# Decode attention beside a GEGLU FFN on one core: cache tiles of four heads in 64 KB rows, two overlapping key places and one value place

## The chip, the cores and the metric

The kernel runs on one core of a Trainium2 chip. The metric is the device time of one execution in microseconds (us). Before the change it is 1317.43 us, the median of three runs (1317.10 to 1317.47). A core has a matmul engine (PE, with its weight loads shown apart as PEld), a vector engine (DVE), an activation engine (ACT), a general engine (POOL) and a queue engine (SP) which here issues every transfer. Sixteen DMA engines carry a transfer together, each its own share of the rows. SBUF is the on-chip memory of 128 partitions, PSUM the small memory that PE writes.

## What is computed

One decode step with a batch of 4: attention over a cache, beside a gated FFN, mixed by a gate. Everything is float32.

```
q  = (x @ wq) as (4, 32 heads, 128)           # x: 4 x 512, wq: 512 x 4096
s  = q . k_cache / sqrt(128)                  # k_cache: 4 x 32 x 4096 x 128
p  = softmax(s)                               # over the 4096 cached positions
a  = (p . v_cache as 4 x 4096) @ wo           # v_cache like k_cache, wo: 4096 x 512
b  = (gelu_tanh(x @ w_gate) * (x @ w_up)) @ w_down    # F = 1792
g  = sigmoid(sum(x * gate_w))
out = g * a + (1 - g) * b                     # 4 x 512
```

The two caches are 268 MB each. All weights together are 28 MB. Every byte is read once.

## The kernel before

**Tiles.** A tile of the cache is two heads (`HT = 2`) of one batch row: 2 x 4096 positions x 128 numbers, 4 MiB. It lies as 128 partitions of 32 KB; a partition holds `R = 64` consecutive positions of one head, which are one contiguous run in memory. There are `NT = 64` key tiles and 64 value tiles. Group `g` is the pair of heads, `b = i % 4` the batch row of tile `i`.

**Buffers.** A pool `kv` of `NB = 5` buffers of 32 KB per partition holds everything that is streamed: `wq` (two halves), key and value tiles, the FFN's weights and `wo`. `load` (L62 to L79) takes the next buffer and issues one transfer on SP, so a transfer waits until the last reader of what lay in that buffer five loads earlier is done. The list `loads` (L81 to L86) fixes the order: `wq` halves, key 0, then key `i+1` and value `i` in turn. `w_gate` and `w_up` come behind values 19 and 20 (`FFN_AT = 20`), `wo`'s first half ahead of the last three value tiles, `w_down` and `wo`'s second half (in three pieces, `WO_END`) at the very end.

**One tile's work (main loop, L310 to L347).** Keys: DVE multiplies the tile by the query, spread over all partitions (`products`, L190, in two halves of 128 x 4096 numbers), and sums each position's 128 products (`sums`, L194); then it takes the maximum of each partition (`max_a`, L201) and PE turns that column into a row (L203). One tile later `soft_max` (L206 to L217) takes the maximum of each head (L208), spreads it with a small matmul (L210), and ACT computes the exponentials into `PM` (L215), an array with zeros around the weights of each head. `pv` (L228) multiplies values by these weights on PE: 16 matmuls of 128 x 512, each of which runs as two passes, into a PSUM tile `PO`. After four tiles `gather` (L240) copies `PO`, sums its parts and the denominators with small matmuls; `weigh` (L253) divides; once per 16 heads `turn` and `turned` (L261, L269) bring the result into the layout that `project_a` (L278) multiplies with `wo`.

**Order.** The schedule is written by hand: each engine runs its instructions in program order, and each waits for semaphores of the others. In tile `i` the program takes the next load of the list after `sums(i)` and again after `pv(i-1)`; each is issued once its buffer is free. `ffn_up` and `ffn_gelu` run inside tiles 20 and 21, `project_a(0)` in tile 62. After the loop come the last softmax and `pv`, `gather`, `weigh`, `turn`, `turned`, `ffn_down` with `w_down`, `project_a(1)` with `wo`'s second half, the mixing by the gate (L360) and the store (L361).

**Start.** PE needs `x` and the first half of `wq` for the queries (L147); DVE picks each partition's head and batch row from the result (L162 to L166), `q_spread` (L174) spreads a group's query over the partitions.

Of the kernel before, what the change touches and what calls it, by code (L numbers as in the profile page):

```python
# [17 lines left out]
def tile_gated_mix(ctx: ExitStack, tc: tile.TileContext, x, kc, vc, wq, wo, w_gate, w_up, w_down, gate_w, out):  # L18
    nc = tc.nc
# [6 lines left out]
    HT = 2  # L26
    PH = P // HT
    R = S // PH
    NT = B * H // HT
    NB = 5  # L30
    TW = R * D
    RJ = 4
    RA = R // 2
    FFN_AT = 20
# [3 lines left out]
    E = HW * D // P  # L38
    WO_END = (0, 10, 14, E)
# [7 lines left out]
    sel = head.tile([P, RJ, B, HT], F32)  # L47
    t1 = head.tile([P, E * B], F32)
    qd = head.tile([P, D], F32)
    xT = head.tile([P, KC, 4, B, 8], F32)  # L50
    kv = ctx.enter_context(tc.tile_pool(name="kv", bufs=NB))
# [7 lines left out]
    T = {}  # L59

    def load(kind, i):
        t = T[kind, i] = kv.tile([P, TW], F32, name="kv")  # L62
        if kind in "kv":
            h, b = HT * (i // B), i % B
            src = (kc if kind == "k" else vc)[b, h:h + HT].rearrange("h (p r) d -> (h p) (r d)", p=PH)
            n = 2 if (kind, i) == ("v", NT - 1) else 1
            for s in range(n):
                nc.sync.dma_start(t[:, s * TW // n:(s + 1) * TW // n], src[:, s * TW // n:(s + 1) * TW // n])
        elif kind == "q":
            nc.sync.dma_start(t, wq.rearrange("(p c) n -> p (c n)", c=KC)[:, i * TW:(i + 1) * TW])  # L70
        elif kind == "f":
            nc.sync.dma_start(t[:, :KC * F], (w_gate, w_up)[i].rearrange("(p c) n -> p (c n)", c=KC))
        elif kind == "d":
            nc.sync.dma_start(t[:, :FC * DM], w_down.rearrange("(p i) n -> p (i n)", i=FC))
        else:
            src = wo[i * HW * D:(i + 1) * HW * D].rearrange("(p e) n -> p (e n)", e=E)
            ends = WO_END if i else (0, E)
            for e0, e1 in zip(ends, ends[1:]):
                nc.sync.dma_start(t[:, e0 * DM:e1 * DM], src[:, e0 * DM:e1 * DM])  # L79

    loads = [("q", 0), ("q", 1), ("k", 0)]  # L81
    for i in range(NT - 2):
        loads += [("k", i + 1), ("v", i)]
        if i in (FFN_AT - 1, FFN_AT):
            loads.append(("f", i - FFN_AT + 1))
    loads[-1:] = [("k", NT - 1), ("w", 0)] + [("v", i) for i in range(NT - 3, NT)] + [("d", 0), ("w", 1)]  # L86
    loads = iter(loads)

    def load_next():
        n = next(loads, None)  # L90
        if n:
            load(*n)

    load_next()
    x_sb = consts.tile([B, DM], F32)
    nc.sync.dma_start(x_sb, x.rearrange("b s d -> (b s) d"))
    load_next()
    for _ in range(NB - 2):
        load_next()
# [5 lines left out]

    for j in range(RJ):
        nc.vector.tensor_reduce(sel[:, j], ident.rearrange("p (c b m) -> p b m c", c=4, b=B)[:, :, HT * j:HT * (j + 1), :],
                                axis=AX.X, op=OP.add)


    PZ = 32 - RJ * HT
# [15 lines left out]
    def gate():  # L127
        z = ps2.tile([P, 1], F32, name="sm")
        for c in range(KC):
            nc.tensor.matmul(z, xT[:, c, :], gw[:, c:c + 1], start=c == 0, stop=c == KC - 1)  # L130
        ez = work.tile([P, 1], F32, name="m1")
        nc.scalar.activation(ez, z, AF.Exp, scale=-1.0)
        gd = work.tile([P, 1], F32, name="nb")
# [8 lines left out]
    for c in range(KC):  # L142
        w = T["q", c // 2].rearrange("p (c n) -> p c n", c=2)[:, c % 2, :]
# [6 lines left out]
    u = consts.tile([P, 2, 512], F32)  # L150
# [9 lines left out]
    nc.vector.tensor_reduce(hmask, ident.rearrange("p (j b a) -> p j a b", j=4, b=B), axis=AX.X, op=OP.add)  # L160
    for s in range(2):
        nc.vector.tensor_tensor(u[:, s].rearrange("p (a d) -> p a d", d=D), PO[s],  # L162
                                amask[:, s * HB:(s + 1) * HB, None].to_broadcast([P, HB, D]), op=OP.mult)
# [4 lines left out]
    for _ in range(2):  # L168
        load_next()
# [17 lines left out]
    def products(i, r0, r1):  # L187
        g, b = divmod(i, B)
        t = T["k", i].rearrange("p (r d) -> p r d", d=D)[:, r0:r1]
        nc.vector.tensor_tensor(t, t, QB[g][:, b:b + 1, :].to_broadcast([P, r1 - r0, D]), op=OP.mult)  # L190

    def sums(i):
        SC[i] = work.tile([P, R], F32, name="sc")
        nc.vector.tensor_reduce(SC[i], T["k", i].rearrange("p (r d) -> p r d", d=D), axis=AX.X, op=OP.add)  # L194

# [32 lines left out]
    def pv(i, j0=0, j1=R // RJ):  # L228
        g, b = divmod(i, B)
        N, n = RJ * D, R // RJ  # L230
        for j in range(j0, j1):
            c, m0 = j % 4, PZ + 32 * j - RJ * HT * b
            nc.tensor.matmul(PO[g % 2][32 * c:32 * c + 32].rearrange("p j d -> p (j d)"), PM[i % 2][:, m0:m0 + 32],  # L233
                             T["v", i][:, j * N:(j + 1) * N], start=b == 0 and j < 4, stop=b == B - 1 and j >= n - 4)

    OS, OT = {}, {}

    def gather(g):  # L240
        o = work.tile([P, RJ, D], F32, name="o", bufs=1)
        nc.scalar.activation(o, PO[g % 2], AF.Copy)  # L242
        OS[g] = ps2.tile([B * HT, D + 1], F32, name="sm")
        for j in range(RJ):
            nc.tensor.matmul(OS[g][:, :D], sel[:, j].rearrange("p b h -> p (b h)"), o[:, j, :],  # L245
                             start=j == 0, stop=j == RJ - 1)
# [3 lines left out]

    ONA = consts.tile([B * HT, E, HW // HT, HT, D // E], F32)

    def weigh(g):  # L253
        ri = work.tile([B * HT, 1], F32, name="ri")
        nc.vector.reciprocal(ri, OS[g][:, D:])  # L255
        nc.vector.tensor_scalar(ONA[:, :, g % (HW // HT)],  # L256
                                OS[g][:, :D].rearrange("p (k e) -> p e k", e=E)[:, :, None, :]
# [3 lines left out]
    def turn(w):  # L261
        OT[w] = ps1.tile([P, E, B, HT], F32, name="oT")
        for e in range(E):
            nc.tensor.transpose(OT[w][:, e].rearrange("p b h -> p (b h)"), ONA[:, e].rearrange("q g h k -> q (g h k)"),  # L264
                                ident[:B * HT, :B * HT])

    OTS = {}

    def turned(w):  # L269
        t = work.tile([P, E * B, HT], F32, name="tm", bufs=1)  # L270
        nc.vector.tensor_tensor(t, OT[w].rearrange("p e b h -> p (e b) h"),
                                pmask[:, None, :].to_broadcast([P, E * B, HT]), op=OP.mult)
        nc.vector.tensor_tensor(t1, t[:, :, 0], t[:, :, 1], op=OP.add)
        OTS[w] = work.tile([P, E, 32], F32, name="ot", bufs=1)
        nc.scalar.activation(OTS[w].rearrange("p e (b k) -> p (e b) k", k=8), t1[:, :, None].to_broadcast([P, E * B, 8]),
                             AF.Copy)

    def project_a(w):  # L278
        for e in range(E):
            project(a_acc, OTS[w][:, e, :], T["w", w][:, e * DM:(e + 1) * DM], (w, e) == (0, 0),  # L280
# [3 lines left out]
    hT = consts.tile([P, FC, 32], F32)  # L284

    def ffn_up(s):
        ps = ps1.tile([P, FG], F32, name="q")
        for c in range(KC):
            for j in range(4):
                nc.tensor.matmul(ps[32 * j:32 * j + 32, :], xT[:, c, :32],  # L290
                                 T["f", s][:, c * F + j * FG:c * F + (j + 1) * FG], start=c == 0, stop=c == KC - 1)
        nc.scalar.activation(u[:, s, :FG], ps, AF.Copy)

    def ffn_gelu():
        x1 = u[:, 0, :FG]
        s = T["f", 1].rearrange("p (a n) -> p a n", n=512)
        t1, t2, t3, th, y, v = (s[:, a, :FG] for a in range(6))
# [5 lines left out]
        nc.vector.scalar_tensor_tensor(v, y, 0.5, u[:, 1, :FG], op0=OP.mult, op1=OP.mult)  # L303
# [4 lines left out]
    def ffn_down():  # L308
        w = T["d", 0].rearrange("p (f n) -> p f n", n=DM)
        for f in range(FC):  # L310
            project(b_acc, hT[:, f, :], w[:, f, :], f == 0, f == FC - 1)


    q_spread(0)
    for i in range(NT):
        g, b = divmod(i, B)
        pair = i > B and i % B == 1
        products(i, 0, RA)
        if i > 0:
            soft_max(i - 1)  # L320
        if pair:
            weigh(g - 1)
        products(i, RA, R)
        sums(i)
        load_next()
        if i > 0:
            pv(i - 1)
            load_next()
# [3 lines left out]
        if pair and g % (HW // HT) == 0:  # L332
            turn(g // (HW // HT) - 1)
            turned(g // (HW // HT) - 1)
        if i == 2:
            nc.sync.dma_start(gw, gate_w.rearrange("(p c) -> p c", c=KC))
        if i == 6:
            gate()
        if i + B < NT and b == 1:
            q_spread(g + 1)  # L340
        if i in (FFN_AT, FFN_AT + 1):
            ffn_up(i - FFN_AT)
            if i == FFN_AT + 1:
                ffn_gelu()
            load_next()
        if i == NT - 2:
            project_a(0)  # L347
            load_next()
# [9 lines left out]
    project_a(H // HW - 1)  # L358
# [25 lines left out]
```

## Time and profile before

| | before |
|---|---|
| median of three runs | 1317.43 us |
| profiled execution, its own time | 1317.39 us |
| span of the profiled execution, first to last instruction | 1315.5 us |
| instructions | 7385 |
| read from HBM | 564.67 MB |
| DVE busy | 1165.0 us (89%) |
| PE busy | 500.1 us (38%) |
| ACT busy | 90.5 us (7%) |
| granted PE clock, mean | 0.651 |

The page of the profile cuts the span into 40 slices with a digit for each engine's busy share. It lists the DMA queues, the chain of work that ended last (each step followed back to what released it), and the costliest groups of instructions with the mean duration and the idle time before them. Other views are the timeline of a stretch (start, duration, engine, line, operation, and in brackets the idle time of the engine before it and what ended that), the waits of an engine or of SP's queue, and the DMA part for a stretch. Times in the text are from the start of the span.

### The profile page before, as it was taken

The numbers are of one execution on the slowest core, as the hardware profiler recorded it, in microseconds if no ns is written. First come the engines' busy times: TensorE is split into PE (matmuls) and PEld (weight loads), VectorE is DVE, ScalarE is ACT, GpSimd is POOL, SyncE is SP. The second block draws the span as 40 slices with busy tenths as digits, with TensorE's granted clock in tenths as the row PEclk, the third lists the DMA queues.
The fourth block names the chain that finished last, engine by engine and source line by source line (L and its number), as shares of the span: only waits on it lengthen the run. The fifth ranks groups of instructions, "written<-read, shape, count | busy, mean of one in ns | idle before, by whom it ended". The sixth has DMA issues, their size and how long they took to land.

```text
span 1315.5 us, 7385 instructions
## 1 busy us (share of the span) xinstructions
PE 500.1 (38%) x3004; PEld 164.5 (13%) x3004; DVE 1165.0 (89%) x402; ACT 90.5 (7%) x359; POOL 0.7 (0%) x6
## 2 busy tenths in 40 slices
PE   3243443343334334334425433443433432442326
PEld 0011111011111111101111111111111110110113
DVE  2999999999999689999999999999999999999963
ACT  0000000000000000000000000000000000000001
POOL 0000000000000000000000000000000000000000
PEclk9556766666676766566566566657657666666658
DMA  9999999999999999999999999999999999999997
GB/s 410 435 430 430 430 433 438 435 430 431 431 434 434 437 431 432 430 434 435 432 434 430 431 434 435 434 432 430 431 434 433 437 429 430 434 434 433 431 430 334
DMA packets 20076, 565.14 MB, mean 430 GB/s; under 512 B 2360, under 2 KB 2376, under 8 KB 2508
## 3 DMA queue, kind: packets, MB, share of 16 engines
q1 hardware_dynamic: 20044, 564.69, 99.5%
q8 instruction: 23, 0.38, 0.1%
q14 instruction: 9, 0.07, 0.0%
HBM read 564.67 MB, written 0.01 MB: 429 GB/s over the span
## 4 chain that ended last, share of the span: by engine, by line
DMA 61%; DVE 36%; PE 2%; issue 1%; ACT 0%; SPq 0%; DVEq 0%; ACTq 0%
DMA kv<-in_A_k_cache 58%; DVE sc L194 17%; DVE kv L190 17%; DMA kv<-in_A_v_cache 2%; PE po L233 1%; DVE m L201 0%; DVE m L208 0%; PE q L290 0%; PE a_acc L226 0%; DVE ONA L256 0%; PE b_acc L226 0%; PE oT L264 0%; PE sm L203 0%; PE q L178 0%; DVE hT L306 0%
## 5 line engine op out<-in xcount | busy, mean ns | idle before, releaser
L190 DVE TENSOR_TENSOR kv<-kv,qb 128x4096 f32<-128x4096 f32 x128 | 564.8, 4413 | 76.4 <-DMA kv<-in_A_k_cache 76.4
L194 DVE TENSOR_REDUCE sc<-kv 128x64 f32<-128x8192 f32 x64 | 555.9, 8686 | 6.3
L233 PE MATMUL po<-kv,pm 128*32 128x512 f32 x2048 | 372.2, 892 | 283.6 <-DMA kv<-in_A_v_cache 277.7
L210 PE MATMUL sm<-m,ones 1*128 1x2 f32 x128 | 37.1, 357 | 320.4 <-DVE m L208 320.4
L233 PEld LDWEIGHTS po<-kv,pm 128*32 128x32 f32 x2048 | 92.4, 155 | 506.9 <-issue 500.5
L203 PE MATMUL sm<-ident,m 128*1 128x128 f32 x64 | 19.0, 297 | 175.3 <-DVE m L201 175.1
L210 PEld LDWEIGHTS sm<-m,ones 1*128 1x128 f32 x128 | 31.6, 305 | 352.2 <-DVE m L208 346.5
L212 ACT ACTIVATE nb<-sm 128x2 f32<-128x2 f32 x64 | 11.0, 172 | 803.3 <-PE sm L210 803.3
L215 ACT ACTIVATE pm<-sc,nb 64x64 f32<-64x64 f32 x128 | 44.5, 348 | 3.0 <-ACT nb L212 0.2
L203 PEld LDWEIGHTS sm<-ident,m 128*1 128x1 f32 x64 | 5.1, 79 | 223.2 <-issue 121.5
L208 DVE TENSOR_REDUCE m<-sm 1x2 f32<-1x128 f32 x64 | 17.4, 272 | 13.1 <-PE sm L203 13.1
L178 PE MATMUL q<-QM,hmask 128*64 128x512 f32 x64 | 25.4, 885 | 3.4 <-DVE QM L166 3.4
L182 ACT ACTIVATE qb<-q 128x512 f32<-128x512 f32 x16 | 9.6, 597 | 226.6 <-PE q L178 226.6
L215 ACT ACTIVATION_READ_ACCUMULATOR pm<-sc,nb 64x1 f32 x128 | 23.6, 185 | 0.0
L245 PE MATMUL sm<-o,sel 128*8 128x128 f32 x128 | 16.6, 273 | 11.4 <-ACT o L242 11.4
L242 ACT ACTIVATE o<-po 128x512 f32<-128x512 f32 x16 | 9.6, 597 | 141.4 <-PE po L233 141.4
L201 DVE TENSOR_REDUCE m<-sc 128x1 f32<-128x64 f32 x64 | 14.1, 220 | 2.2
L245 PEld LDWEIGHTS sm<-o,sel 128*8 128x8 f32 x128 | 10.2, 89 | 28.6 <-ACT o L242 26.8
L255 DVE RECIPROCAL ri<-sm 8x1 f32<-8x1 f32 x16 | 2.3, 147 | 10.1 <-PE sm L247 10.1
L147 PE MATMUL po<-kv,xT 128*32 128x512 f32 x64 | 9.0, 716 | 3.5 <-DMA kv<-in_A_wq 3.1
L123 DVE COPY xT<-sm 128x128 f32<-128x128 f32 x4 | 0.9, 284 | 10.6 <-PE sm L120 10.6
L162 DVE TENSOR_TENSOR u<-po,amask 128x512 f32<-128x512 f32 x2 | 1.4, 691 | 9.9 <-PE po L147 9.9
(52 smaller groups left out, 75.8 us busy)
## 6 DMA issues: line engine op xcount, KB each, us to landing
kv<-in_A_k_cache SPq DMA_DIRECT2D x64, 4096.0 KB, 39.7
kv<-in_A_v_cache SPq DMA_DIRECT2D x63, 4096.0 KB, 30.6
kv<-in_A_wq SPq DMA_DIRECT2D x2, 4096.0 KB, 16.4
kv<-in_A_wo SPq DMA_DIRECT2D x1, 4096.0 KB, 39.8
kv<-in_A_v_cache SPq DMA_DIRECT2D x2, 2048.0 KB, 27.9
kv<-in_B_w_gate SPq DMA_DIRECT2D x1, 3584.0 KB, 38.6
kv<-in_B_w_up SPq DMA_DIRECT2D x1, 3584.0 KB, 28.2
kv<-in_B_w_down SPq DMA_DIRECT2D x1, 3584.0 KB, 22.1
```

What stands on the lines that cost most here:

```text
L178: nc.tensor.matmul(ps[h * PH:(h + 1) * PH].rearrange("p b d -> p (b d)"), hmask[:, j, a:a + 1].to_broadcast([P, PH]), QM.rearrange("p b d ...
L182: nc.scalar.activation(QB[g], ps, AF.Copy)
L190: nc.vector.tensor_tensor(t, t, QB[g][:, b:b + 1, :].to_broadcast([P, r1 - r0, D]), op=OP.mult)
L194: nc.vector.tensor_reduce(SC[i], T["k", i].rearrange("p (r d) -> p r d", d=D), axis=AX.X, op=OP.add)
L201: nc.vector.tensor_reduce(m1, SC[i], axis=AX.X, op=OP.max)
L203: nc.tensor.transpose(MT[i], m1, ident)
L208: nc.vector.tensor_reduce(m2, MT[i].rearrange("o (h p) -> o h p", h=HT), axis=AX.X, op=OP.max)
L210: nc.tensor.matmul(nbp, ones[:1, :], m2, start=True, stop=True)
L212: nc.scalar.activation(nb, nbp, AF.Copy, scale=-scale)
L215: nc.scalar.activation(PM[i % 2][:, PZ:].rearrange("p (c m) -> p c m", m=32)[s, :, h:RJ * HT:HT], SC[i][s, :].rearrange("p (c j) -> p c j" ...
L233: nc.tensor.matmul(PO[g % 2][32 * c:32 * c + 32].rearrange("p j d -> p (j d)"), PM[i % 2][:, m0:m0 + 32], T["v", i][:, j * N:(j + 1) * N], ...
L245: nc.tensor.matmul(OS[g][:, :D], sel[:, j].rearrange("p b h -> p (b h)"), o[:, j, :], start=j == 0, stop=j == RJ - 1)
```

## The change

A tile is now four heads of one batch row (`HT = 4`): 8 MiB, 128 partitions of 64 KB, `R = 128` positions per partition, `NT = 32` tiles of each kind. `wq` comes as one transfer, in rows of 64 KB too.

The pool of five buffers is gone. One array `big` of 176 KB per partition has fixed places: even key tiles at 0 to 64 KB, odd key tiles at 48 to 112 KB, values at 112 to 176 KB. The two key places share 16 KB, a quarter of a tile. So `products` and `sums` are each cut into a shared quarter, which is done first (128 x 4096 products), and the other three quarters (128 x 12288). Key `i+1` is issued as soon as the shared quarter of tile `i` is summed. Value `i` is issued when `pv(i-1)` is done. `wq` lies in the values' place at the start; then `w_gate` and `w_up` lie there, issued behind key 0 and used inside tile 0 (`ffn_up`, `ffn_gelu`), and value 0 is issued after that. The last value tile goes into the first key place. `wo`'s first half and `w_down` go into the values' place after the value tile before the last, `wo`'s second half into the second key place; all of them are issued behind the last value tile. `project_a(0)` moves from tile 62 to the end, ahead of the last `turn`.

`PO` now gathers two tiles (`BP = 2`), since a tile has four heads and a matmul's 32 columns hold two batch rows of them; `gather_a` copies it after every second tile and `gather` sums both copies after every fourth. `turn` and `turned` run once per group of four heads, on 32 partitions, into a quarter of `T1`; `spread` makes the operand of `project_a` out of it, once per 16 heads.

```diff
-    HT = 2
+    HT = 4
-    NT = B * H // HT
-    NB = 5
+    NG = H // HT
+    NT = B * NG
+    RO = R // 4
+    BP = 2
-    kv = ctx.enter_context(tc.tile_pool(name="kv", bufs=NB))
+    kv = ctx.enter_context(tc.tile_pool(name="kv", bufs=1))
...
+    KB_, VA = TW - RO * D, 2 * TW - RO * D
+    big = kv.tile([P, VA + TW], F32)
+    Q0, F0, F1, W0, D0 = VA, VA, VA + KC * F, VA, VA + TW // 2
+    W1, ES = TW, TW + TW // 2
+    def place(a, n):
+        return big[:, a:a + n]
+    def K(i):
+        return place(KB_ * (i % 2), TW)
+    def V(i):
+        return place(VA if i < NT - 1 else 0, TW)
+    def load_kv(src, i, dst):
+        nc.sync.dma_start(dst, src[i % B, HT * (i // B):HT * (i // B) + HT].rearrange("h (p r) d -> (h p) (r d)", p=PH))
...
+    nc.sync.dma_start(place(Q0, KC * H * D), wq.rearrange("(p c) n -> p (c n)", c=KC))
+    x_sb = place(VA - 2 * DM, DM)[:B]
     nc.sync.dma_start(x_sb, x.rearrange("b s d -> (b s) d"))
+    load_k(0)
...
+    def rows(i, shared):
+        return ((R - RO, R), (0, R - RO))[not shared] if i % 2 == 0 else ((0, RO), (RO, R))[not shared]
+    def products(i, shared):
         g, b = divmod(i, B)
-        t = T["k", i].rearrange("p (r d) -> p r d", d=D)[:, r0:r1]
+        r0, r1 = rows(i, shared)
+        t = K(i).rearrange("p (r d) -> p r d", d=D)[:, r0:r1]
         nc.vector.tensor_tensor(t, t, QB[g][:, b:b + 1, :].to_broadcast([P, r1 - r0, D]), op=OP.mult)
...
+    load_f(0)
+    load_f(1)
     q_spread(0)
     for i in range(NT):
         g, b = divmod(i, B)
-        products(i, 0, RA)
+        products(i, True)
         if i > 0:
             soft_max(i - 1)
-        products(i, RA, R)
-        sums(i)
-        load_next()
+        if i > B and b == 1:
+            turned(g - 1)
+        sums(i, True)
+        if i < NT - 1:
+            load_k(i + 1)
+        else:
+            load_v(i)
+        products(i, False)
+        if i == 0:
+            ffn_up(0)
+            ffn_up(1)
+            ffn_gelu()
+            load_v(0)
+        sums(i, False)
         if i > 0:
             pv(i - 1)
-            load_next()
+            if i < NT - 1:
+                load_v(i)
+            if i % BP == 0:
+                gather_a(i - 1)
             if b == 0:
                 gather(g - 1)
         max_a(i)
+        if i > 0 and b == 0:
+            weigh(g - 1)
+            turn(g - 1)
...
+    load_w(0)
+    load_d()
+    load_w(1)
+    spread(0)
     soft_max(NT - 1)
     pv(NT - 1)
-    gather(H // HT - 1)
-    weigh(H // HT - 1)
-    turn(H // HW - 1)
-    turned(H // HW - 1)
+    gather_a(NT - 1)
+    gather(NG - 1)
+    weigh(NG - 1)
+    project_a(0)
+    turn(NG - 1)
+    turned(NG - 1)
+    spread(1)
     ffn_down()
```

More of the change, by code (lines that the diff above doesn't have):

```diff
@@ L46, in tile_gated_mix @@
     ones = head.tile([P, P], F32)
-    sel = head.tile([P, RJ, B, HT], F32)
-    t1 = head.tile([P, E * B], F32)
-    qd = head.tile([P, D], F32)
+    sel = head.tile([P, RJ, 3, BP * HT], F32)
+    T1 = [head.tile([P, E * B], F32, name=f"t1{w}") for w in range(H // HW)]
     xT = head.tile([P, KC, 4, B, 8], F32)
-    kv = ctx.enter_context(tc.tile_pool(name="kv", bufs=NB))
+    kv = ctx.enter_context(tc.tile_pool(name="kv", bufs=1))
     consts = ctx.enter_context(tc.tile_pool(name="consts", bufs=1))
@@ L56, in tile_gated_mix @@
     ctx.enter_context(tc.manual_schedule())
[L59 to L92, printed above, removed]
-    load_next()
-    x_sb = consts.tile([B, DM], F32)
+    KB_, VA = TW - RO * D, 2 * TW - RO * D
@@ new lines, in load_v, with load_f, load_d, load_w @@
+    def load_v(i):
+        load_kv(vc, i, V(i))
+    def load_f(s):
+        nc.sync.dma_start(place((F0, F1)[s], KC * F), (w_gate, w_up)[s].rearrange("(p c) n -> p (c n)", c=KC))
+    def load_d():
+        nc.sync.dma_start(place(D0, FC * DM), w_down.rearrange("(p i) n -> p (i n)", i=FC))
+    def load_w(w):
+        t = place((W0, W1)[w], E * DM)
+        src = wo[w * HW * D:(w + 1) * HW * D].rearrange("(p e) n -> p (e n)", e=E)
+        ends = WO_END if w else (0, E)
+        for e0, e1 in zip(ends, ends[1:]):
+            nc.sync.dma_start(t[:, e0 * DM:e1 * DM], src[:, e0 * DM:e1 * DM])
@@ L132, in gate @@
         nc.scalar.activation(ez, z, AF.Exp, scale=-1.0)
-        gd = work.tile([P, 1], F32, name="nb")
+        gd = work.tile([P, 1], F32, name="gd")
         nc.vector.tensor_scalar(gd, ez, 1.0, None, op0=OP.add)
@@ L185, in tile_gated_mix, with sums @@
     SC = {}
-    def products(i, r0, r1):
+    def rows(i, shared):
+        return ((R - RO, R), (0, R - RO))[not shared] if i % 2 == 0 else ((0, RO), (RO, R))[not shared]
+    def products(i, shared):
         g, b = divmod(i, B)
-        t = T["k", i].rearrange("p (r d) -> p r d", d=D)[:, r0:r1]
+        r0, r1 = rows(i, shared)
+        t = K(i).rearrange("p (r d) -> p r d", d=D)[:, r0:r1]
         nc.vector.tensor_tensor(t, t, QB[g][:, b:b + 1, :].to_broadcast([P, r1 - r0, D]), op=OP.mult)
-    def sums(i):
-        SC[i] = work.tile([P, R], F32, name="sc")
-        nc.vector.tensor_reduce(SC[i], T["k", i].rearrange("p (r d) -> p r d", d=D), axis=AX.X, op=OP.add)
+    def sums(i, shared):
+        if shared:
+            SC[i] = work.tile([P, R], F32, name="sc")
+        r0, r1 = rows(i, shared)
+        nc.vector.tensor_reduce(SC[i][:, r0:r1], K(i).rearrange("p (r d) -> p r d", d=D)[:, r0:r1], axis=AX.X, op=OP.add)
     MT = {}
@@ L226, in project, with pv, gather_a @@
             nc.tensor.matmul(acc[32 * c:32 * c + 32, :], t, w[:, c * C4:(c + 1) * C4], start=start, stop=stop)
-    def pv(i, j0=0, j1=R // RJ):
-        g, b = divmod(i, B)
+    def pv(i):
+        b = i % BP
         N, n = RJ * D, R // RJ
-        for j in range(j0, j1):
+        for j in range(n):
             c, m0 = j % 4, PZ + 32 * j - RJ * HT * b
-            nc.tensor.matmul(PO[g % 2][32 * c:32 * c + 32].rearrange("p j d -> p (j d)"), PM[i % 2][:, m0:m0 + 32],
-                             T["v", i][:, j * N:(j + 1) * N], start=b == 0 and j < 4, stop=b == B - 1 and j >= n - 4)
-    OS, OT = {}, {}
+            nc.tensor.matmul(PO[i // BP % 2][32 * c:32 * c + 32].rearrange("p j d -> p (j d)"), PM[i % 2][:, m0:m0 + 32],
+                             V(i)[:, j * N:(j + 1) * N], start=b == 0 and j < 4, stop=b == BP - 1 and j >= n - 4)
+    O, OS, OT = {}, {}, {}
+    def gather_a(i):
+        O[i // BP] = work.tile([P, RJ, D], F32, name="o")
+        nc.scalar.activation(O[i // BP], PO[i // BP % 2], AF.Copy)
     def gather(g):
-        o = work.tile([P, RJ, D], F32, name="o", bufs=1)
-        nc.scalar.activation(o, PO[g % 2], AF.Copy)
         OS[g] = ps2.tile([B * HT, D + 1], F32, name="sm")
-        for j in range(RJ):
-            nc.tensor.matmul(OS[g][:, :D], sel[:, j].rearrange("p b h -> p (b h)"), o[:, j, :],
-                             start=j == 0, stop=j == RJ - 1)
+        N = B // BP
+        for n in range(N):
+            m0 = BP * HT * (1 - n)
+            for j in range(RJ):
+                nc.tensor.matmul(OS[g][:, :D], sel[:, j, m0:m0 + B * HT], O[N * g + n][:, j, :],
+                                 start=(n, j) == (0, 0), stop=(n, j) == (N - 1, RJ - 1))
         nc.tensor.matmul(OS[g][:, D:], RS[g % 2].rearrange("p b h -> p (b h)"), ones[:, :1], start=True, stop=True)
-    ONA = consts.tile([B * HT, E, HW // HT, HT, D // E], F32)
+    ONA = consts.tile([B * HT, E, HT, D // E], F32)
     def weigh(g):
@@ L255, in weigh, with turn @@
         nc.vector.reciprocal(ri, OS[g][:, D:])
-        nc.vector.tensor_scalar(ONA[:, :, g % (HW // HT)],
-                                OS[g][:, :D].rearrange("p (k e) -> p e k", e=E)[:, :, None, :]
+        nc.vector.tensor_scalar(ONA, OS[g][:, :D].rearrange("p (k e) -> p e k", e=E)[:, :, None, :]
                                 .to_broadcast([B * HT, E, HT, D // E]), ri, None, op0=OP.mult)
-    def turn(w):
-        OT[w] = ps1.tile([P, E, B, HT], F32, name="oT")
+    def turn(g):
+        OT[g] = ps1.tile([32, E, B, HT], F32, name="oT")
@@ L263, in turn, with turned @@
         for e in range(E):
-            nc.tensor.transpose(OT[w][:, e].rearrange("p b h -> p (b h)"), ONA[:, e].rearrange("q g h k -> q (g h k)"),
+            nc.tensor.transpose(OT[g][:, e].rearrange("p b h -> p (b h)"), ONA[:, e].rearrange("q h k -> q (h k)"),
                                 ident[:B * HT, :B * HT])
-    OTS = {}
[L269 to L275, printed above, removed]
+    def turned(g):
+        t = work.tile([32, E * B, HT], F32, name="tm", bufs=1)
+        nc.vector.tensor_tensor(t, OT[g].rearrange("p e b h -> p (e b) h"),
+                                pmask[:32, None, :].to_broadcast([32, E * B, HT]), op=OP.mult)
+        w, r = divmod(g, GW)
+        nc.vector.tensor_reduce(T1[w][32 * r:32 * r + 32], t, axis=AX.X, op=OP.add)
@@ L290, in ffn_up @@
                 nc.tensor.matmul(ps[32 * j:32 * j + 32, :], xT[:, c, :32],
[L291 to L292 removed]
+                                 place((F0, F1)[s] + c * F + j * FG, FG), start=c == 0, stop=c == KC - 1)
+        nc.scalar.activation(fu[:, s, :FG], ps, AF.Copy)
     def ffn_gelu():
[L295 to L297 removed]
+        x1 = fu[:, 0, :FG]
+        t1, t2, t3, th, y, v = (place(F1 + a * DM, FG) for a in range(6))
         nc.vector.tensor_tensor(t1, x1, x1, op=OP.mult)
@@ L331, in tile_gated_mix @@
         max_a(i)
[L332 to L335, printed above, removed]
+        if i > 0 and b == 0:
+            weigh(g - 1)
+            turn(g - 1)
+        if i == 1:
             nc.sync.dma_start(gw, gate_w.rearrange("(p c) -> p c", c=KC))
-        if i == 6:
+        if i == 3:
             gate()
-        if i + B < NT and b == 1:
+        if b == 1 and g + 1 < NG:
             q_spread(g + 1)
[L341 to L348, printed above, removed]
+    load_w(0)
+    load_d()
+    load_w(1)
+    spread(0)
     soft_max(NT - 1)
     pv(NT - 1)
-    gather(H // HT - 1)
-    weigh(H // HT - 1)
-    turn(H // HW - 1)
-    turned(H // HW - 1)
+    gather_a(NT - 1)
[5 more added lines that the diff above has]
+    spread(1)
     ffn_down()
@@ L357, in tile_gated_mix @@
     nc.vector.tensor_scalar(tb, b_acc, g_cols[:, 1:2], None, op0=OP.mult)
-    project_a(H // HW - 1)
+    project_a(1)
     res = work.tile([P, C4], F32, name="res")
```

39 lines of the change are left out of this document (20 added, 19 removed).

## The prediction

> **What bounds the kernel now.** First the page: its DMA slices, its DMA queues and the chain that ended last.
>
> ```profile
> DMA  9999999999999999999999999999999999999997
> q1 hardware_dynamic: 20044, 564.69, 99.5%
> DMA 61%; DVE 36%; PE 2%; issue 1%; ACT 0%; SPq 0%; DVEq 0%; ACTq 0%
> L190 DVE TENSOR_TENSOR kv<-kv,qb 128x4096 f32<-128x4096 f32 x128 | 564.8, 4413 | 76.4 <-DMA kv<-in_A_k_cache 76.4
> L194 DVE TENSOR_REDUCE sc<-kv 128x64 f32<-128x8192 f32 x64 | 555.9, 8686 | 6.3
> ```
>
> The sixteen DMA engines carry packets 99.5% of the span. The chain holds 36% DVE because a buffer freed by DVE lets SP issue, but DVE idles 76.4 us waiting for keys, so DVE doesn't set the end. Next the timeline of a late stretch: DVE and PE starting the moment a tile lands.
>
> ```profile
> 1205.45 4.43 DVE L190 TENSOR_TENSOR kv<-kv,qb 128x4096 f32<-128x4096 f32 x1 [1.42 <-DMA kv<-in_A_k_cache]
> 1215.15 5.58 PE L233 MATMUL po<-kv,pm 128*32 128x512 f32 x32 [4.45 <-DMA kv<-in_A_v_cache]
> 1224.76 4.42 DVE L190 TENSOR_TENSOR kv<-kv,qb 128x4096 f32<-128x4096 f32 x1 [1.33 <-DMA kv<-in_A_k_cache]
> ```
>
> Key, value, key: 1224.76 - 1205.45 = 19.31 us for 8 MiB, 434.4 GB/s. That is the floor: one new tile every 19.3 us, a key and a value every 38.6. Third, the DMA part for 100 to 400 us (rows of 32 KB) and for 1306 to 1311 us (`wo`'s pieces, short rows):
>
> ```profile
> q1 hardware_dynamic: 4592, 129.77, 100.3%
> ...
> q1 hardware_dynamic: 186, 0.91, 43.5%
> ```
>
> Columns: packets, MB, share of 16 engines. Last, the end of the timeline:
>
> ```profile
> 1305.44 3.26 PE L226 MATMUL b_acc<-kv,hT 128*32 128x128 f32 x112
> 1308.52 3.68 PE L226 MATMUL a_acc<-kv,ot 128*32 128x128 f32 x128
> 1312.27 0.35 DVE L360 SCALAR_TENSOR_TENSOR res<-a_acc,g_cols,tb 128x128 f32<-128x128 f32 x1 [3.14 <-PE a_acc L226]
> ```
>
> `wo`'s last piece is issued at 1283.6 and lands 27.1 us later (section 6 of the page for such pieces), at 1310.7. PE ends at 1312.2, 1.5 us behind it.
>
> The profiled execution took 1317.39 us, 1.9 beyond its span and 0.04 from the median, so sums against it hold for the runs.
>
> **The change, part by part.**
>
> *Bytes.* The same 564.67 MB, at the floor already. DVE, PE or ACT work saved inside the stream is worth nothing; what counts is time per byte, gaps in the stream, and its two ends.
>
> *Longer rows, fewer transfers.* 131 transfers of cache and `wq` become 65. Each gives an engine 8 rows and one semaphore packet, so an engine handles 528 rows and 66 semaphores fewer: 594 packets. Their price, from the two DMA parts: 4592 packets and 129.77 MB took 100.3% of 16 x 300 = 4814 us; 186 and 0.91 MB took 43.5% of 80 = 34.8 us. Solved for a time per packet and per byte: 6.8 ns per packet, 27.1 GB/s per engine. The upper bound is 594 x 0.0068 = 4.0 us. But 16 engines at 27.1 are 434 GB/s, which the key-to-key step reaches with its packets included, and a share above 100% means that packets overlap. So the lower bound is 0 (no row of the trace hints at a loss from merging two adjoining rows). Both rows are equally near: I take the middle, -2.0.
>
> *Spacing.* Sixteen engines now read addresses that lie 64 KB x 4 apart, not 32 KB x 4. The nearest row: before, each half of `wq` was read as 32 KB out of rows spaced 64 KB. PE's wait for the second half ends at 22.53 us and the first key tile's consumer starts at 32.19, a step of 9.66 like any other, and `x`, queued behind the first half, is there at 13.05: halves 9.5 apart. Cost taken: 0. The Trainium skill, DMA: Bandwidth & Descriptors, Latency and other measured facts, says that copies whose rows lie at large powers of two slow down, 207 GB/s at 512 KiB against 214 unhindered and 103 at 4 MiB. By it a pitch doubled to 64 KiB is a step that way, by an amount it doesn't state (the 3% of its 512 KiB figure would be 39 us, an estimate from that page). The trace disagrees at 64 KB.
>
> *Lookahead.* Five 4 MiB buffers allowed about three queued transfers. Now key `i+1` waits for `sums` of the shared quarter of tile `i`, value `i` for `pv(i-1)`; the queue holds the running transfer and at most one or two behind. Would it run dry? An issue needs 2.3 us to flow (shortest issue-to-landing of the buffers' loads 12.0, less 9.66).
> Key `i+1`: the quarter takes 4.4 of products, 0.2 of L208 and 8.69/2 = 4.35 of sums, so it is issued 8.9 us after key `i` lands and flows at 11.2; value `i-1` runs until 19.3. Slack 8 us.
> Value `i`: `pv` has twice the passes. 32 passes took 5.6 us above, at half clock 6.4; 64 take at most 13.7. PE starts when value `i-1` lands, and the exponentials are ready by then (key landing + 4.4 + about 2.5, 12 us early). Issued at 13.8, flowing at 16.1; key `i+1` runs until 19.3. Slack 3 us at the worst clock, 7 otherwise.
> DVE per tile: 4 x 4.41 + 2 x 8.69 + 0.3 + 0.2 = 35.5 us, plus 1.6 every fourth tile for `weigh` and `turned` (L255 and L256, 0.6, with twice the columns, and two short operations), under 38.6. Cost 0; if the cover went, the next value or key tile would be late.
>
> *Start.* `x` now lies behind all of `wq`, 22.4 us instead of 13. The query matmuls took 5.4 + 3.6 = 9.0 us and the steps to QB 5.1 more (26.2 to 31.3); with 1 us ahead of them QB is ready at 38, key 0 lands at 32.1 + 9.66 = 41.8. Hidden, 4 us to spare.
> The FFN weights (8.5 us each) follow key 0 and land at 58.7; SP is held by `wq`'s matmuls until 33, before 41.8. In tile 0 DVE does 8.8 + 13.2 of products, gelu about 5.4 and the other sums 13.1, until about 82.7, while key 1 lands at 78.0. DVE starts tile 1 4.7 us late, key 2 is issued at 91.7 and flows at 94; value 0 lands at 97.3. No gap; DVE gains 3 us per tile and has caught up by tile 3. Cost 0. In tiles 20 and 21 the FFN's DVE work goes: gain 0, the stream hid it.
>
> *End.* Behind the last value tile come 27.8 us of `wo`, `w_down` and `wo`. In them PE does `pv` (9 to 13.7), waits for the 0.6 copy, gathers (2.1), does `project_a(0)` (3.7), `turn` (1.2) and `ffn_down` (3.3): 20 to 25 us. It stands idle when `wo`'s second half lands, 3.7 us before the end, so behind the last piece only two of 16 blocks remain, 3.68/8 = 0.5 us instead of 1.5 (with the wait, 0.6): -0.9. At half clock PE would end later than before: bound +1.
>
> *Sum:* -2.0 - 0.9 = -2.9, so 1314.5 us; the bounds are 1317.4 - 4.9 = 1312.5 and 1317.4 + 1 = 1318.4.
>
> **The rivals.**
> *Nothing moves.* Rows save nothing (the DMA hardware may cut them into 32 KB packets again; the 434.4 GB/s speak for it), the end gains little or nothing: 1316 to 1318.5.
> *The queue runs dry (slower).* Place: value `i`'s issue. If `pv` with its wait ends more than 17 us after value `i-1` lands, every value tile starts late by the excess. From that point each microsecond costs 31; 0.2 us means 1321, 0.5 us means 1330. For it: only 3 us of worst-case slack, and a timeline that shows no load issued this late. Against it: half-clock passes are all counted in it, and the second half of a long run goes at full clock in the rows above.
> *The rows' spacing slows the reads.* The mechanism is the engines' streams falling on the same part of memory; every 1% of rate is 13 us, 1330 at one. Against it: the step of 9.66 with 64 KB spacing. The Trainium skill's rule on row pitch (DMA: Bandwidth & Descriptors, Latency and other measured facts) would bring this about.
>
> **How the numbers follow.** Forecast 0.62, nothing moves 0.16, dry queue 0.15, spacing 0.07. This kernel's measurement can tell about 0.2%, 2.6 us: faster means under 1314.8. The forecast case reaches it when the rows save at least 1.7 of their 4.0, three times in four: 0.46 faster, 0.16 same. The second rival adds 0.16 to same; the last two are the slower 0.22. The predicted time is the forecast's, 1314.5. The range goes from 1312 (half below the sum's bound) to 1324, which takes in the milder dry queue and leaves out some 0.15 of the chance.
>
> **What would show it.** Right: about 65 fewer landings, packets of 65536 bytes (packets on q1 near 11,000), the landing step of two tiles under 38.6 us, DVE still waiting for keys in nearly every tile, the last block of `wo` ending about 0.6 us after its landing. Wrong: packets still near 20,000 (rows cut); DMA slices below 9, or SP waiting for `pv` while the DMA share of a stretch falls below 0.99 (dry); a full share at under 430 GB/s (spacing); DVE without waits for keys (DVE the bound).

## The result, and the profile after

The changed kernel takes 1314.03 us, the median of eleven runs (1313.84 to 1314.50), against 1317.28 us for the kernel before on the same chip (1316.86 to 1317.59). The ratio is 0.9976, with a 95% interval from 0.9967 to 0.9985: 0.24% faster. The profiled execution took 1313.86 us, its span is 1312.1 us.

The page of the changed kernel: DMA slices, the main DMA queue, the chain that ended last, the two groups of DVE.

```profile
DMA  9999999999999999999999999999999999999997
q1 hardware_dynamic: 10540, 564.68, 99.4%
DMA 73%; DVE 26%; issue 1%; SPq 0%; PE 0%; ACT 0%; DVEq 0%
L198 DVE TENSOR_TENSOR big<-big,qb 128x4096 f32<-128x4096 f32 x64 | 555.8, 8684 | 96.7 <-DMA big<-in_A_k_cache 96.7
L204 DVE TENSOR_REDUCE sc<-big 128x32 f32<-128x4096 f32 x64 | 555.5, 8679 | 1.3
```

The transfers are still the bound. The packets fell from 20044 to 10540 for the same bytes, so rows of 64 KB do travel as one packet. DVE still waits for keys, 96.7 us instead of 76.4: with half as many tiles it waits less often and longer. (A mean of 8684 ns mixes the shared quarter with the three other quarters.)

The timeline of the changed kernel, around two awaited keys. SP's lines are issues.

```profile
195.64 4.43 DVE L198 TENSOR_TENSOR big<-big,qb 128x4096 f32<-128x4096 f32 x1 [0.88 <-DMA big<-in_A_k_cache]
204.61 0.33 SPq L76 DMA_DIRECT2D big<-in_A_k_cache  x1
215.05 9.10 PE L243 MATMUL po<-big,pm 128*32 128x512 f32 x64 [14.09 <-DMA big<-in_A_v_cache]
224.20 0.33 SPq L76 DMA_DIRECT2D big<-in_A_v_cache  x1
234.23 4.43 DVE L198 TENSOR_TENSOR big<-big,qb 128x4096 f32<-128x4096 f32 x1 [2.64 <-DMA big<-in_A_k_cache]
```

Key to key is 38.59 us for 16 MiB. The next key is issued 9.0 us after a key lands (the prediction had 8.9), the next value 9.15 us after a value lands, as soon as `pv` is done.

The DMA part of the changed kernel for 100 to 400 us, and the end of its timeline:

```profile
q1 hardware_dynamic: 2364, 129.76, 99.9%
```

```profile
1304.53 3.43 PE L236 MATMUL a_acc<-big 128*32 128x128 f32 x112 [1.52 <-DMA big<-in_A_wo]
1308.12 0.64 PE L236 MATMUL a_acc<-big 128*32 128x128 f32 x16 [0.15 <-DMA big<-in_A_wo]
1308.83 0.35 DVE L390 SCALAR_TENSOR_TENSOR res<-a_acc,g_cols,tb 128x128 f32<-128x128 f32 x1 [5.39 <-PE a_acc L236]
```

The queue's share is 99.9% where it was 100.3%: the same bytes cost less DMA time. At the end PE waits for `wo` and is done 0.7 us after the last piece, where it needed 1.5 before.

The gain of the profiled span, 1315.5 - 1312.1 = 3.4 us, lies in two places. The last piece of `wo` landed at 1310.7 and lands at 1308.1: 2.6 us come out of the stream. The work behind it, up to the mixing on DVE, shrank from 1.6 us (1312.27 - 1310.7) to 0.8.

That the stream as a whole runs faster also shows between the first key tile's work and the last key that DVE waits for. Before, from 32.19 to 1244.18 us, 62 keys, 61 values and 7 MiB of FFN weights landed: 124.75 loads of 4 MiB, 9.715 us each. After, from 42.19 to 1241.64, 31 keys, 30 values and the same weights: 123.75 such units, 9.693 us each. The difference, 0.022 us, times all 134.6 units of 4 MiB is 3.0 us.

Where in the stream it lies shows in the landings: the kept traces hold one for each load and each of the sixteen engines. The first engine to land a load takes 9.681 us per 4 MiB before and 9.660 after, as the median of all steps and as their mean. So the gain is spread over every step: 0.021 us times 134.6 is 2.8 us.

### The profile page after: what moved, and what is told of

Its sections match the earlier page's. It is cut to its first block, busy times and chain, and to the rows that moved or that the text cites. A ratio compares the mean times of both kernels' runs of the same rounds, so it can differ in the third digit from the quotient of the medians.

```text
span 1312.1 us, 6886 instructions
## 1 busy us (share of the span) xinstructions
PE 392.1 (30%) x2988; PEld 136.4 (10%) x2988; DVE 1148.8 (88%) x271; ACT 91.9 (7%) x319; POOL 0.7 (0%) x6
## 3 DMA queue, kind: packets, MB, share of 16 engines
q1 hardware_dynamic: 10540, 564.68, 99.4%
## 4 chain that ended last, share of the span: by engine, by line
DMA 73%; DVE 26%; issue 1%; SPq 0%; PE 0%; ACT 0%; DVEq 0%
DMA big<-in_A_k_cache 70%; DVE sc L204 13%; DVE big L198 12%; DMA big<-in_A_wo 2%; DVE m L218 0%; DVE t L285 0%; DVE tm L282 0%; DVE hT L324 0%; PE a_acc L236 0%; DVE big L318 0%; DVE big L321 0%; DVE big L320 0%; DVE big L316 0%; ACT big L319 0%; DVE m L211 0%
## 5 line engine op out<-in xcount | busy, mean ns | idle before, releaser
L198 DVE TENSOR_TENSOR big<-big,qb 128x4096 f32<-128x4096 f32 x64 | 555.8, 8684 | 96.7 <-DMA big<-in_A_k_cache 96.7
L204 DVE TENSOR_REDUCE sc<-big 128x32 f32<-128x4096 f32 x64 | 555.5, 8679 | 1.3
L243 PE MATMUL po<-big,pm 128*32 128x512 f32 x2048 | 295.0, 741 | 438.4 <-DMA big<-in_A_v_cache 435.9
L243 PEld LDWEIGHTS po<-big,pm 128*32 128x32 f32 x2048 | 80.9, 133 | 626.2 <-issue 623.7
L220 PE MATMUL sm<-m,ones 1*128 1x4 f32 x64 | 18.7, 360 | 207.3 <-DVE m L218 207.3
L225 ACT ACTIVATE pm<-sc,nb 32x128 f32<-32x128 f32 x128 | 67.4, 526 | 2.5
L220 PEld LDWEIGHTS sm<-m,ones 1*128 1x128 f32 x64 | 15.9, 306 | 225.7 <-DVE m L218 219.2
L225 ACT ACTIVATION_READ_ACCUMULATOR pm<-sc,nb 32x1 f32 x128 | 26.2, 205 | 0.0
L181 PE MATMUL q<-QM,hmask 128*32 128x512 f32 x64 | 14.6, 1004 | 3.5 <-DVE QM L171 3.5
L260 PE MATMUL sm<-o,sel 128*16 128x128 f32 x128 | 15.6, 273 | 0.0
L269 DVE RECIPROCAL ri<-sm 16x1 f32<-16x1 f32 x8 | 1.2, 147 | 13.7 <-PE sm L262 13.7
```

The source lines that it names most:

```text
L181: nc.tensor.matmul(ps[h * PH:(h + 1) * PH].rearrange("p b d -> p (b d)"), hmask[:, j, a:a + 1].to_broadcast([P, PH]), QM.rearrange("p b d ...
L204: nc.vector.tensor_reduce(SC[i][:, r0:r1], K(i).rearrange("p (r d) -> p r d", d=D)[:, r0:r1], axis=AX.X, op=OP.add)
L220: nc.tensor.matmul(nbp, ones[:1, :], m2, start=True, stop=True)
L225: nc.scalar.activation(PM[i % 2][:, PZ:].rearrange("p (c m) -> p c m", m=32)[s, :, h:RJ * HT:HT], SC[i][s, :].rearrange("p (c j) -> p c j" ...
L243: nc.tensor.matmul(PO[i // BP % 2][32 * c:32 * c + 32].rearrange("p j d -> p (j d)"), PM[i % 2][:, m0:m0 + 32], V(i)[:, j * N:(j + 1) * N] ...
L260: nc.tensor.matmul(OS[g][:, :D], sel[:, j, m0:m0 + B * HT], O[N * g + n][:, j, :], start=(n, j) == (0, 0), stop=(n, j) == (N - 1, RJ - 1))
```

## The experiments

Times are medians; "before" on the chips of these runs was 1317.2 to 1317.4 us. A landing is that of the last engine in the run's one profiled execution.

**One transfer cut by columns: 32 KB rows again.**

```diff
-        nc.sync.dma_start(dst, src[...])
+        s = src[...]
+        for c in range(2):
+            nc.sync.dma_start(dst[:, c * TW // 2:(c + 1) * TW // 2], s[:, c * TW // 2:(c + 1) * TW // 2])
```

> The changed kernel with every cache tile and wq loaded as two transfers of column halves, so packets are 32 KB again; places, order and end stay. Theory (fewer packets): the 594 packets per engine come back and with them the 2.0 to 2.7 us of the stream, 1316.0 to 1316.7 us. Rival (the fixed places and the order of the loads gave the gain): no change, 1314.0.

1317.15 us (1316.86 to 1318.40), ratio to before 0.9999 (0.9990 to 1.0008). All but a trace of the gain is gone though places, order and loads stay: 3.1 us hang on the cut. An engine handles 520 rows and 65 semaphores more, 585 packets, so at most 5.3 ns each. Not all of it is the stream's: `wo`'s last piece lands at 1310.9, 2.8 us later than in the changed kernel, which is 4.9 ns a packet. The rest lies behind that landing:

```profile
1307.42 4.94 PE L240 MATMUL a_acc<-big 128*32 128x128 f32 x128 [2.89 <-DMA big<-in_A_wo]
1312.43 0.35 DVE L394 SCALAR_TENSOR_TENSOR res<-a_acc,g_cols,tb 128x128 f32<-128x128 f32 x1 [7.48 <-PE a_acc L240]
```

PE was granted half its clock from 1307.3 to 1310 here (0.50 in the windows of this stretch, 1.00 in the changed kernel) and ended 1.4 us behind the landing instead of 0.7.

**Cut into four: 16 KB rows.** The same edit with `range(4)` and quarters.

> The changed kernel with every cache tile and wq loaded as four transfers of column quarters, packets of 16 KB. Theory (a fixed time per packet): three times what the 32 KB rows lose, 6 to 8 us, 1320 to 1322. Rival (packets overlap, and their fixed time shows in no sum): 1314 to 1315.

1322.59 us (1322.35 to 1322.73), ratio 1.0039 (1.0027 to 1.0052). A further 1170 packets per engine cost 5.4 us, 4.6 ns each. By the landings (1316.7 here) it is 5.0 ns, so the price is close to linear in the packets. The DMA part for 100 to 400 us, first with rows of 32 KB, then with 16 KB:

```profile
q1 hardware_dynamic: 4600, 129.77, 100.3%
```

```profile
q1 hardware_dynamic: 9009, 129.11, 100.6%
```

The share rises with the packets while the bytes stand still or fall.

**Rows or transfers? First try, halves of the partitions.**

```diff
+        for c in range(2):
+            nc.sync.dma_start(dst[c * P // 2:(c + 1) * P // 2], s[c * P // 2:(c + 1) * P // 2])
```

> The changed kernel with every cache tile loaded as two transfers of 64 partitions each: twice the transfers, the same 64 KB rows. Theory (rows count): only the semaphore packets come back, at most 0.6 us, 1314.0 to 1314.6. Rival (the number of transfers counts, not the rows): all of the stream's gain goes, 1316.0 to 1316.7.

2658.53 us, ratio 2.018 (2.015 to 2.020). Neither theory had this: a transfer of 64 partitions runs at half the rate. The DMA part for 600 to 1200 us:

```profile
DMA packets 2392, 125.00 MB, mean 208 GB/s; under 512 B 480, under 2 KB 480, under 8 KB 480
q1 hardware_dynamic: 2386, 124.91, 100.2%
```

The engines are busy all the time and move 208 GB/s instead of 433. So the run says nothing on its question. The Trainium skill, SBUF — State Buffer, section "Door 1: The DMA port swizzle", states that partitions 0 to 63 reach only 8 of the memory's 16 DMA ports and puts the ceiling there at about 218 GB/s; the trace agrees, at 208.

**Rows or transfers? Second try, one transfer of 32 KB rows.**

```diff
-        ...rearrange("h (p r) d -> (h p) (r d)", p=PH)
+        s = src[...].rearrange("(c h) (p r) d -> (h p) c (r d)", c=2, p=2 * PH)
+        nc.sync.dma_start(dst.rearrange("q (c n) -> q c n", c=2), s)
```

> The changed kernel with one transfer per cache tile, as in the change, but each partition filled by two separate runs of 32 KB (partition p gets the p-th run of the tile's first 4 MiB and of its second), so packets are 32 KB. Part of the keys and values then stand under the weights of other heads, which leaves the work and its time alone but not the output's meaning. wq stays in 64 KB rows. Theory (rows count): 512 more packets of about 5 ns, 2.6 us, 1316.4 to 1317.1, like the run with two column halves. Rival (the number of transfers counts): 1314.0.

1316.40 us (1316.21 to 1316.78), ratio 0.9993 (0.9984 to 1.0001). With as many transfers as the changed kernel, 2.4 us of the gain are gone: 512 more packets per engine, 4.6 ns each. It is the rows, not the transfers. (The landing, 1310.5, gives 4.6 ns too.) Here the rows lie 32 KB apart again, so this run doesn't separate their spacing from their length; the next one does.

**The end alone, in the kernel before.**

```diff
-    loads[-1:] = [("k", NT - 1), ("w", 0)] + [("v", i) for i in range(NT - 3, NT)] + [("d", 0), ("w", 1)]
+    loads[-1:] = [("k", NT - 1)] + [("v", i) for i in range(NT - 3, NT)] + [("w", 0), ("d", 0), ("w", 1)]
...
     weigh(H // HT - 1)
+    project_a(0)
     turn(H // HW - 1)
```

> The kernel before with the changed kernel's end alone: wo's first half is loaded behind the last value tile instead of three value tiles ahead of it, and project_a(0) stands ahead of the last turn. Theory: PE is idle when wo's last piece lands and only two blocks remain, 0.7 to 0.9 us faster than before, 1316.5. Rival (the end gives nothing; all of the gain is the stream's): 1317.3.

1316.75 us (1316.50 to 1316.98) against 1317.43 (1317.05 to 1317.87). The ranges don't touch, though the ratio's interval, 0.9986 to 1.0003, includes one: 0.7 us, likely but not beyond the noise. The end of its timeline:

```profile
1307.52 4.20 PE L226 MATMUL a_acc<-kv,ot 128*32 128x128 f32 x128 [0.46 <-DMA kv<-in_A_wo]
1311.79 0.35 DVE L358 SCALAR_TENSOR_TENSOR res<-a_acc,g_cols,tb 128x128 f32<-128x128 f32 x1 [4.30 <-PE a_acc L226]
```

The whole of `project_a(1)` now follows a wait for `wo`; before, it followed `ffn_down`.

This kernel and the one with 32 KB rows in the new places have nearly the same packets (9 per engine apart) and the same loads at the end. They differ in the places, the lookahead and the spacing of the rows (32 KB here, 64 KB there). `wo`'s last piece lands at 1311.0 here and 1310.9 there, and the first engine takes 9.68 us per 4 MiB in both: none of the three shows a cost in the stream. The medians are 0.4 us apart (1316.75 and 1317.15), but in the two profiled executions that kind of difference lies behind the last landing, in the half-clock matmuls above, and outside the span (2.0 us there, 1.8 here).

**Less lookahead: the key places overlap by half a tile.**

```diff
-    RO = R // 4
+    RO = R // 2
```

> The changed kernel with key places that overlap by half a tile (32 KB per partition) instead of a quarter; the operand of project_a gets a buffer of its own. Key i+1 is then issued 17.7 us after key i lands (8.8 of products, 0.2, 8.7 of sums) and flows 2.3 us later, at 20.0, while value i-1 ends at 19.3. Theory (the queue runs dry from that point): 0.7 us per tile, 31 tiles, about 1336. Rival (there is more cover than I counted, as the DVE would otherwise be the next bound only at 38.6): 1314.

1384.16 us (1380.19 to 1387.93), ratio 1.0501 (1.0473 to 1.0529). It runs dry, at three times the price expected. The main queue's line, the issue-to-landing line for keys (last column, us), and the timeline:

```profile
q1 hardware_dynamic: 10540, 564.68, 95.9%
big<-in_A_k_cache SPq DMA_DIRECT2D x32, 23.0
```

```profile
329.73 8.69 DVE L198 TENSOR_TENSOR big<-big,qb 128x8192 f32<-128x8192 f32 x1 [6.67 <-DMA big<-in_A_k_cache]
347.24 0.33 SPq L76 DMA_DIRECT2D big<-in_A_k_cache  x1
349.45 8.78 PE L243 MATMUL po<-big,pm 128*32 128x512 f32 x64 [10.20 <-DMA big<-in_A_v_cache]
...
370.29 8.69 DVE L198 TENSOR_TENSOR big<-big,qb 128x8192 f32<-128x8192 f32 x1 [5.44 <-DMA big<-in_A_k_cache]
```

The key is issued 17.5 us after the last one landed, as expected. But it lands 23.0 us after its issue, and 19.3 of these are transfer: 3.7 us more than its own transfer, where 2.3 were expected, although the value ahead of it was still landing for 2.2 of them (349.45 - 347.24). So the gap is 17.5 + 3.7 - 19.3 = 1.9 us per tile, 59 us in 31 tiles, against some 70 measured. In every fourth tile, behind `turned`, the issue comes 18.4 us after the landing, which adds 0.9 us each time; the last few microseconds are not accounted for. The 3.7 us are not a fixed cost of a start: `wq`, which finds the queue empty at the beginning, lands 22.1 us after its issue, 2.8 more than the 19.3.

**In between: three eighths.** `RO = 3 * R // 8`.

> The changed kernel with key places that overlap by three eighths of a tile (24 KB per partition). Key i+1 is issued 13.4 us after key i lands and flows at 15.7, 3.6 us ahead of the end of value i-1. Theory (cover is enough up to 19.3): no change, 1313.7 to 1314.5. Rival (every loss of lookahead costs something, through engines that run ahead of the slowest): some us more, 1316 or above.

1315.10 us (1314.52 to 1317.69), ratio 0.9985 (0.9976 to 0.9994). With 3.7 us in place of 2.3 the slack here is 19.3 - 13.4 - 3.7 = 2.2 us. A slack above zero was not enough: about 1 us is lost, and the spread is larger. The rival's mechanism fits: the sixteen engines don't stand at the same point of the stream. In the changed kernel their common share falls off over some 8 us at the end (columns of the windows: stretch, length, busy times, granted clock, DMA share, GB/s):

```profile
1300.00:1304.00 4.00, 3.01 (x88) 2.64 (x80) 0.35 (x1) 0.00 (x0) 0.00 (x0) 0.85 0.94 392
1304.00:1308.00 4.00, 3.43 (x112) 2.96 (x112) 0.00 (x0) 0.00 (x0) 0.00 (x0) 1.00 0.45 184
```

The engines' landings say how far apart they are: for the last full tiles the first engine of the changed kernel is 4.6 us ahead of the last, and in this run's profiled execution, the slowest of its ten, 2.4. An engine that leads by more than the slack runs dry first: 2.2 us of slack would hold the leaders back, and the changed kernel's 6.4 us would leave a lead of 4.6 alone. The numbers fit this; that the lost microsecond comes from it is argued, not shown.

**Can instruction traffic separate the engines?** 4096 memsets on the idle POOL.

```diff
+    idle = consts.tile([P, 1], F32)
+    for _ in range(4096):
+        nc.gpsimd.memset(idle, 0.0)
```

> The changed kernel with 4096 memsets of 128 x 1 on POOL, which is idle otherwise; nothing waits for them. Theory (instruction fetches are carried by the same 16 DMA engines, and each packet of 16 KB holds one engine for about 1.5 us while the slowest engine sets the end): about 16 more packets on the instruction queue, 1 to 6 us more if they are spread over the engines, 1315 to 1320. Rival (work on an idle engine is free): 1314.0.

1332.07 us (1331.49 to 1332.95), ratio 1.0112 (1.0097 to 1.0128): 18 us for work that nothing waits for. The page's two instruction queues (packets, MB, share):

```profile
q8 instruction: 23, 0.38, 0.1%
q14 instruction: 38, 0.31, 0.1%
```

The changed kernel has 23 and 6 there: 32 packets of 8 KB more, 0.56 us each. The memsets run until 640 us. While they do, awaited keys come 40 us apart instead of 38.6:

```profile
160.35 4.43 DVE L198 TENSOR_TENSOR big<-big,qb 128x4096 f32<-128x4096 f32 x1 [4.86 <-DMA big<-in_A_k_cache]
200.27 4.42 DVE L198 TENSOR_TENSOR big<-big,qb 128x4096 f32<-128x4096 f32 x1 [2.00 <-DMA big<-in_A_k_cache]
240.20 4.43 DVE L198 TENSOR_TENSOR big<-big,qb 128x4096 f32<-128x4096 f32 x1 [3.98 <-DMA big<-in_A_k_cache]
```

DVE's operations are as long as before (4.43 us), so it is the transfers that are slower. My 1 to 6 us took the packets as spread over the engines. The landings show otherwise: from 215 us on, fifteen engines land a tile within 3 us of each other, and the sixteenth follows alone, 5 to 8 us behind them while the memsets run (433.1 and 440.5 us for one tile). Such a lag can't come about in one tile, which takes 0.7 us more than its 19.3, so it is one engine that falls behind, and the slowest engine sets a tile's landing. That the instruction packets hold it up fits their number, but each costs 0.56 us where 8 KB at 27 GB/s an engine (433 / 16) would take 0.30, an estimate; the memsets' own writes were not separated from the fetches. The Trainium skill, Runtime: NRT & Kernel Launch, Instruction fetch mechanics, calls the cost of crossing a block of instructions mostly hidden; if the fetches are the cause, this kernel, bound by its transfers, doesn't hide it: the run lost 18 us.

**Fewer instructions on PE.**

```diff
-        for c in range(4):
-            nc.tensor.matmul(acc[32 * c:32 * c + 32, :], t, w[:, c * C4:(c + 1) * C4], start=start, stop=stop)
+        nc.tensor.matmul(acc, t, w, start=start, stop=stop)
```

> The changed kernel with project writing one PSUM tile of 32 x 512 in one matmul per block instead of four of 128 columns in four column groups: 184 matmuls instead of 736 passes on PE, at 107 ns a pass against 4 x 29. Theory (PE's instructions come in packets of 16 KB on the DMA engines, and fewer of them delay the slowest engine less): 19 of such packets instead of 23, 0 to 1.5 us less in the stream, about 0.6; the end loses some 0.3 on the mixing of 32 x 512 numbers: 1312.8 to 1314.3. Rival (no link): 1314.3.

1337.10 us (1336.75 to 1337.98), ratio 1.0151 (1.0137 to 1.0165). Both theories missed it: the end became PE's.

```profile
1292.25 13.90 PE L235 MATMUL a_acc<-big 128*32 128x512 f32 x32
1306.58 12.20 PE L235 MATMUL b_acc<-big,hT 128*32 128x512 f32 x28
1318.62 13.90 PE L235 MATMUL a_acc<-big 128*32 128x512 f32 x32
```

One pass takes 13.90/32 = 0.43 us, at a full granted clock, where I had counted 0.107. That shorter time is `pv`'s at full clock, where four passes in turn write four different groups of 32 PSUM partitions (column groups) and take 0.43 us together (in the burst shown above, the weight loads come in fours 0.43 us apart from 219.7 us on); a lone group takes as long for one. The instruction packets fell to 21, and whether that helped the stream can't be read under an end that is 23 us late.

> The changed kernel again, beside the run with fewer matmuls on the same chip: 1314.0, as both theories have it.

1314.14 us (1313.86 to 1314.95), ratio 0.9977 (0.9968 to 0.9986): the result again.

## Why the prediction was right, point by point

The forecast was 1314.5 us, within 0.5 us of the result, and the two gains it named are the two that came. That it came so close is partly luck: the gain of the rows was taken as the middle of two bounds 4 us apart. Term by term:

- **Longer rows**, -2.0 with bounds 0 and -4.0. The term was mis-sized: 2.6 to 2.8 us by the landings (3.1 by the medians of the first experiment, which hold some of the end), 4.6 to 5.0 ns a packet, where the profile's two DMA parts gave 6.8 and the middle of the bounds 3.4. The upper price rests on a small row: half a unit in the last digit of its 0.91 MB moves it by 1.0 ns. What was wrong was the lower bound. It took the step of 19.31 us as a rate at which packets cost nothing, but that step was shorter than most: the median of two loads, from last landing to last landing, is 19.33 us between 100 and 1265 us. And the pace of the first engine shows the packets' price in every step.
- **Spacing**, 0: right. The rows of 64 KB move at 433 GB/s at a share of 99.9%, and the two kernels with 32 KB rows land their last piece within 0.1 us of each other at 32 and at 64 KB of spacing. The loss that the Trainium skill's page DMA: Bandwidth & Descriptors (Latency and other measured facts) states for large powers of two is given there from 512 KiB on; no run here shows one at 64 KB.
- **Lookahead**, 0: right; no cost shows. What was too small is the 2.3 us from issue to flow: a load issued as late as in the run with half a tile of overlap lost 3.7. With that, the slack was 19.3 - 9.0 - 3.7 = 6.6 us for keys and 19.3 - 9.15 - 3.7 = 6.4 for values, not 8 and 7. `pv` took 8.4 to 10.0 us, well under the 13.7 of half clock: in the burst shown above the granted clock is 0.50 up to 218.9 us and 1.00 from 219.4. The kernel keeps well clear of the cliff, but the two runs with a wider overlap show that it is there.
- **Start**, 0: right. The query was spread at 38.2 us (38 forecast) and key 0 used at 42.2. Key 2 was issued at 91.47 (91.7). Key 1 came 1.4 us later than forecast and DVE was 0.2 earlier, so DVE was 3.1 us late at tile 1 and had caught up at tile 2, one tile sooner.
- **End**, -0.9: right. The work behind the last landing shrank by 0.8 us, the end alone gave -0.7, and PE finishes 0.7 us behind the last landing, where 0.6 was forecast. The bound of +1 at half clock is real too: the run with 32 KB rows lost 0.7 us of its profiled execution to it.

In the two profiled executions the stream gave 2.6 us and the end 0.8, together the 3.4 us by which the span shrank. The medians of the four kernels (before, the end alone, 32 KB rows in the new places, changed) give -0.7, +0.4 and -3.1; their sum is the whole gain whatever each of them holds, so it confirms nothing.

Of the rivals, "nothing moves" had the rows wrong. The dry queue is real as a mechanism but not at this overlap. Where it was brought about, its place was the keys' issue; the values' issue, where the rival had it, never came near its worst case.

## What to carry to other kernels

When the DMA engines carry packets all the time and the rate is at its ceiling, there is still a little in the packets: halving their number by doubling contiguous rows gave 0.2%, at about 5 ns a packet and engine. Two DMA parts with rows of different length price that before anything is built, roughly: here they gave 6.8 ns. A buffer plan with less lookahead cost nothing that showed where each load was issued 10 us ahead of the end of the transfer in front of it, about 1 us in all where it was 6 us, and 5% where it was 2. The three runs fit a simple rule, which they don't prove: the lead that is needed is the 3.7 us above plus the engines' spread, here up to 4.6. Compute behind the last landing is worth cutting to the last piece's own share.

## What the runs showed of the hardware that was not expected

- Transfers that cover partitions 0 to 63 and 64 to 127 one after the other moved 208 GB/s, with the queue's packets busy 100.2% of the time, against 433 GB/s for 128 partitions at once.
- 4096 instructions on an idle engine cost a kernel bound by its transfers 18 us: one DMA engine fell 5 to 8 us behind the fifteen others, and the time between awaited keys grew from 38.59 to 39.9 us while they ran.
- A load issued 2 us before the end of the transfer ahead of it landed 23.0 us after its issue, 3.7 us more than its own transfer; one issued into an empty queue 22.1 us after.
- The sixteen DMA engines drift apart in a long stream: the first lands its share of a tile 1.6 us ahead of the last at 118 us and 4.6 us ahead at 1242 us.
- A matmul pass of 128 x 32 weights and 512 columns takes 0.43 us when all passes go to one column group (13.90 us for 32) and 0.107 us when four column groups take turns (0.43 us for four), both at a granted clock of 1.00.
